# A state-space layer and a gated MLP on one core: ten loads move to GpSimd's queue, and TensorE multiplies a constant in gaps that the planner foresees

## The chip, the cores and the metric

The kernel runs on one core of a Trainium2 chip. The core has five engines that run side by side, each with its own queue of instructions: TensorE (PE, matrix products into PSUM), VectorE (DVE), ScalarE (ACT), GpSimd (POOL) and SyncE (SP, which here only issues transfers). Sixteen DMA engines move data. Transfers are issued by SP, ScalarE or GpSimd, and an issue stands in its engine's queue like any other instruction: what is behind it waits for it.

The metric is the time of one execution on the device in microseconds (us), the median of several runs.

## What is computed

An input `u` of 2048 tokens x 448 channels goes through two blocks, each with a layer norm that is scaled and shifted by rows of `silu(c) @ w_mod`:

```python
mod = (silu(c) @ w_mod).reshape(1, 6, 1, -1)          # sa, ca, ga, sb, cb, gb
h = layernorm(x) * (1 + ca) + sa
x = x + ga * S4(h)                                     # long convolution along the tokens
h = layernorm(x) * (1 + cb) + sb
x = x + gb * ((gelu(h @ w_gate) * (h @ w_up)) @ w_down)
# S4: K[d, l] = Re sum_n C[d,n] dB[d,n] exp(dt A)[d,n]^l ; y = irfft(rfft(K) * rfft(u)) + u * Dskip
```

with 448 channels, 256 states and an inner width of 1792.

## The kernel before

The work falls into stages that overlap.

1. **Start** (to about 50 us). `mod_row` multiplies the broadcast `silu(c)` with a third of `w_mod`'s rows at a time: load `fg` by SP (`m.ld`, L763), four matrix products of 448 columns (`m.mm`, L768), copy by ScalarE (`m.ev`, L771). Meanwhile VectorE and ScalarE prepare the first quarter of the kernel's parameters (`prep`), ScalarE stores them as `lh` (`p.put`, L520) and loads them back in another layout as `lt` (`lt0`, `lt1`, L575). The normalised input goes through a first DFT stage (`ua`, L832).
2. **Main stage** (to about 376 us). For 56 groups of channels: exponents and angles as matrix products (`x.mm` L593, `y.mm` L612, `ang`/`anc` L630), exponential and sine on ScalarE, products on VectorE (`tx`, `tyc`, `tys`, L679 to L687), sums on TensorE (`kgen`, L710; `ka`, L735). Between these run the DFT of the input and, by groups of channels, that of the kernel with the product and the way back (`k_fft`).
3. **Last group of the convolution** (376 to 399 us), `t_fft`: `t.fwd` L1069, `t.p0`/`t.p1` L1075 and L1078, `t.inv` L1085, then a copy out of PSUM (`t.z`, by ScalarE or VectorE), a store of `y` (`t.st`, SP, L1093) and loads of it in another layout (`yi.l0` by SP and `yi.l1` by GpSimd, L1154). For the last, small piece the copy goes straight from tile to tile in single rows (`yi.d00` to `yi.d11`, L1166, issued by SP, ScalarE and GpSimd).
4. **The first block of 512 tokens enters the MLP** (399 to 422 us), `conv_out`: `co.mm` L1246/L1251, the residual and the norm's sums on VectorE (`co.add`), `co.n` L1288/L1289, transposition on TensorE (`co.t`, L1294/L1296), and two half-precision parts (`co.h` on ScalarE or VectorE, `co.l`, L1304).
5. **MLP** (422 us to the end). Weights are loaded in blocks of 256 columns (`w.ld`, L1187, 512 KB each, two a block), split in two half-precision parts (`w.hi` L1195 on ScalarE, `w.lo` L1199/L1200 on VectorE), stored for the later blocks of tokens (`wr.st`, L1209) and used (`gu2`, `gu`, L1371/L1365). Then `dn` (L1441, L1472) with the down weights (`d.ld`, L1547).

**The planner.** Nothing is ordered by hand. Each step is a `Task` with a cost on its engine, a due time `v`, the tasks it depends on, and the buffers that it takes and uses. `Plan.order` places the tasks one at a time: it takes the engine that can start something first, and among the tasks that could start there within 0.25 us (at once on ScalarE) the one with the lowest `v`. The result is the program's order for every engine. `LEAD` adds a constant to the due times of each kind of task (several constants share the tasks of a kind out in order), and `LEAN` is what a start on VectorE is made dearer by, where a task may run on ScalarE or VectorE. A transfer ends, in the plan, after all transfers before it at 280 KB a us; it may start only when the eighth transfer before it, of those issued by SP and ScalarE, has ended (`lanes`). At 0.3 us from engine to engine (`HOP`) this gives planned times; the chip only keeps the order.

Three places that the change touches wait for the end of the main stage (`EV["end"]`): the load of the first residual rows (`x1.ld`, L1120), three constants (`c.ai`, `c.id`, `c.ih`, L414) and the first weights. The first three blocks of weights (`PRE = 3`) are allowed before the MLP begins:

```python
gate = EV["end"] if cb < PRE else CO[0][1]
hold = [YO[2, 2]] if cb < 1 else YL      # a store of y; all loads of yi
t1 = add("w.ld", {"SP": 0.42}, v - 3, ld, [EV["end"]] + hold, [wb], kb=540)
```

Of the kernel before, what the change touches and what calls it, by code (L numbers as in the profile page):

```python
# [41 lines left out]
    "c.ai": (71.008,), "c.ak": (31.634,), "c.au": (64.741,), "c.ea": (129.571,), "c.id": (-5.74,), "c.ih": (81.5,),  # L42
    "c.ld": (-70.212,), "c.rd": (36.588,), "co.add": (126.534,), "co.adde": (-479.654,), "co.addl": (177.332,),
    "co.addx": (510.429, 276.254, 263.838, 306.027), "co.c2": (-16.462, 185.363, 68.605, 81.504),
    "co.h": (1287.071, 1321.404), "co.h2": (-57.238, -19.565, -34.416, 62.618), "co.l": (166.825, 99.971),
    "co.l2": (-304.102, -376.884, -381.167, -327.959), "co.mm": (1047.13,), "co.mme": (35.95,),
    "co.mml": (321.391,), "co.mmx": (504.891, 504.282, 510.751, 509.801), "co.n": (-32.018, -300.752),
    "co.nx": (-309.183, -245.328, -200.245, -90.738), "co.rc": (52.991, 384.121), "co.rcx": (915.491,),
    "co.rt": (-12.141, 45.958), "co.rtx": (-618.711,), "co.t": (505.324, 339.683),
    "co.t2": (-464.884, -636.939, -578.467, -639.884),  # L50
    "cos": (-96.053, -141.432, -54.911, -135.117, -68.696, -62.333),
# [6 lines left out]
    "dt": (81.074,), "e.f": (-100.312, 117.922), "e.hi": (227.13, 344.995), "e.ld": (-39.805, -1.088),  # L58
    "e.lo": (8.272, -319.182), "ev.end": (-23.435,), "ev.fp": (-187.94,), "ev.geg": (-67.509,), "ev.ub": (109.206,),
    "f.fc": (-74.649, -73.839, -55.611, 15.224, 63.434, 91.147),  # L60
# [6 lines left out]
    "gu": (497.845, 500.786, 503.249, 509.096, 515.626, 545.649),  # L67
    "gu.g": (-625.109, -552.414, -602.197, -714.965, -686.389, -501.12), "gu.h0": (645.72, 522.69),
    "gu.ha": (-729.389, -596.515, -731.42, -528.62, -704.301, -709.342),
    "gu.hs": (-239.586, -121.625, -135.62, -164.459, -9.293, -189.977), "gu.l0": (-16.693, -130.465),  # L70
    "gu.la": (-265.608, -410.165, -336.957, -514.583, -455.359, -305.327),
    "gu.ls": (191.831, 190.571, 255.197, 314.456, 219.503, 228.103),
    "gu.m": (114.811, 93.18, 25.848, 285.848, 134.211, 151.44),
# [22 lines left out]
    "sin2": (46.891, 86.759, 111.859, -3.781, 88.196, 21.274), "t.fc": (52.17, 4.168), "t.fwd": (-57.224, -139.59),  # L96
    "t.inv": (-32.42, 14.481), "t.p0": (-56.821, 45.808), "t.p1": (-115.221, 1.658, 219.974, -99.911),
    "t.st": (5.684, 132.896), "t.u": (-64.85, -19.41), "t.z": (101.922, 155.786),
    "tx": (-52.929, -36.943, 40.099, -29.624, 27.922, 13.415),
# [5 lines left out]
    "ub.st": (171.069, 76.93), "ub.u": (-80.805, 32.953), "w.hi": (47.827, -108.842, 52.672, -16.405),  # L105
    "w.ld": (-16.684, 35.68, 34.326, 174.065), "w.lo": (33.536, 32.676, -41.147, -28.811), "warm": (-47.271,),
    "wr.ld": (118.569, -172.29, -6.657, 0.537, 11.936, 73.483), "wr.st": (-77.265, -16.436),
    "x.exp": (-46.635, 7.137, 2.518, -127.479, -61.616, -65.308), "x.ld": (-9.142,), "x.ld0": (-42.934,),
    "x.ld1": (-8.964,), "x.mm": (-1.652, -1.606, -1.613, -1.701, -1.664, -1.631), "x1.ld": (17.13, -239.16),
    "y.exp": (29.939, 99.375, 54.648, -1.232, -161.973, 74.141),  # L110
    "y.mm": (-1.933, -1.54, -1.223, -1.275, -1.525, -1.518), "yi.d00": (-147.672,), "yi.d01": (-171.741,),
    "yi.d10": (-130.853,), "yi.d11": (-32.365,), "yi.e": (-88.98,), "yi.l0": (-123.965, 88.548),
    "yi.l1": (-88.669, -10.274), "yi.ld": (196.171,),
}
LEAN = {
# [5 lines left out]
    "t.z": (5.831, 10.31), "ua.ev": (-0.145, -0.075, 0.628, 8.093, -0.059, 1.101),  # L121
# [29 lines left out]
class Plan:  # L151
# [106 lines left out]
    def run(self):  # L258
        for t in self.order():
            t.fn(t.on) if len(t.eng) > 1 else t.fn()  # L260
# [89 lines left out]
def s4_geglu(ctx: ExitStack, tc: tile.TileContext, a: dict, out: bass.AP):  # L350
# [60 lines left out]

    def sp(n, v, dst, src, kb, deps=(), alloc=(), use=(), q="SP"):
        qf = adma if q == "ACT" else dma
        return add(n, {q: 0.42 if q == "SP" else 0.1}, v, lambda: qf(dst(), src()), deps, alloc, use, kb=kb)  # L414
# [168 lines left out]
    def exps(sc, lt):  # L583
        ss = list(range(sc * SUBS, (sc + 1) * SUBS))
        for k in range(0, SUBS, 2):
# [3 lines left out]
            def xmm(grp=grp, pb=pb):  # L589
                pb.tile = gen.tile([128, 1024], FT, name="pg")  # L590
                for m, s in enumerate(grp):
# [10 lines left out]
            t1 = add("x.mm", {"PE": 0.17 * len(grp)}, v, xmm, [lt, c_rd], [pb, mb], [LT[sc]])  # L602
            t2 = add("x.exp", {"ACT": 0.92 if len(grp) > 1 else 0.6}, v, xact, [t1], (), [pb, mb], table=EXP)
# [91 lines left out]
    def kgen(s, deps):  # L695
        m = s // 2
# [3 lines left out]
        def go():  # L700
            if s % 2 == 0:
                KG[m].tile = kgp.tile([128, 4, 128], FT, name="kg")
            kg = KG[m].tile
# [9 lines left out]
        return add("kgen", {"PE": 1.04}, s, go, list(deps) + [KGT.get(s - 1) if s % 2 else None],  # L713
                   [KG[m]] if s % 2 == 0 else [], [TX[s], TY[s]] + ([KG[m]] if s % 2 else []))
# [43 lines left out]
    def mod_row(i, dst, v, sc=1.0, bs=0.0, deps=()):  # L758
# [5 lines left out]

        def mm():
            pb.tile = fft.tile([128, D], FT, name="pf")
            for t in range(4):
                T.matmul(pb.tile, c_sb[:, t:t + 1].to_broadcast([DT, 128]), wb.tile[:, t], start=(t == 0), stop=(t == 3))  # L768
        t1 = add("m.ld", {"SP": 0.42}, v, ldw, deps[2:], [wb], kb=803)
        t2 = add("m.mm", {"PE": 3.22}, v, mm, [t1, t_si], [pb], [wb])  # L770
        return add("m.ev", {"ACT": 0.46}, v, lambda: A.activation(dst, pb.tile, AF.Copy, scale=sc, bias=bs),  # L771
# [42 lines left out]
    def u_norm_a(jb, v, rst):  # L814
        so = {}
        for jj in range(4):
# [11 lines left out]
            def mm(j=j, pbs=pbs):  # L828
                for h in range(2):
                    pbs[h].tile = fft.tile([128, D], FT, name="pf")  # L830
# [292 lines left out]
    def VB(blk):  # L1123
        return 58.5 if blk == 0 else 100.0 + 20.0 * blk - 20.0
# [519 lines left out]
```

## Time and profile before

| | |
|---|---|
| median of 3 runs | 823.77 us (823.62, 823.77, 831.2) |
| the profiled execution, own time | 825.18 us |
| its span (first to last instruction) | 823.4 us |
| mean granted TensorE clock | 0.969 |
| TensorE, VectorE, ScalarE busy | 748.4, 599.6, 470.3 us |
| GpSimd busy | 6.0 us, 14 instructions |
| transfers by SP and ScalarE's queues | 135.4 MB; by GpSimd's 0.26 MB |

Rows of the timeline read: start, duration (of several instructions: from the first to the last), engine, line, operation, output <- input, count, and in brackets the idle time before with what ended it. A name with q (SPq, ACTq) is an issue on that queue. The chain of waits lists start, duration and what the end of the kernel hung on. A table of stages lists busy time and count of each engine, then the granted TensorE clock, the share of the DMA engines and GB/s. Records of fp32 products come two to a product.

### The profile page before, as it was taken

What the parts mean: (1) busy time and instruction counts of PE and PEld (TensorE: products, weight loads), DVE (VectorE), ACT (ScalarE), POOL (GpSimd) and SP (SyncE); (2) the same over time, 40 slices, a digit from 0 to 9 for tenths busy, and PEclk for the clock granted to TensorE, in tenths of its full rate; (3) what the DMA queues carried; (4) which work ended last, traced back from release to release, by engine and by line L of the source; (5) the groups of instructions that cost most, each with busy time, mean ns of one, the idle gap of its engine ahead of it and who ended that gap; (6) DMA issues with size and microseconds to landing.
All of it is one profiled execution on the core that took longest, in us unless ns stands there. A gap on an engine that the chain in (4) does not pass through costs nothing.

```text
span 823.4 us, 19059 instructions
## 1 busy us (share of the span) xinstructions
PE 748.4 (91%) x8166; PEld 461.2 (56%) x8166; DVE 599.6 (73%) x981; ACT 470.3 (57%) x629; POOL 6.0 (1%) x14
## 2 busy tenths in 40 slices
PE   2786789999799999998589999999999999999997
PEld 1344344444577767778466445444496445864477
DVE  7789998999889989897494783178863686244542
ACT  5598999899968999971244553034442353113320
POOL 0000000000000000000200000000000000000000
PEclk9888799999999999999889999999999999999999
DMA  9552369996858846899669756245315322022101
GB/s 283 148 167 92 105 189 236 285 273 200 236 146 257 233 133 193 253 307 295 189 197 298 267 179 179 75 140 166 117 53 146 135 91 90 34 79 90 45 12 35
DMA packets 92526, 136.83 MB, mean 166 GB/s; under 512 B 21280, under 2 KB 75200, under 8 KB 92442
## 3 DMA queue, kind: packets, MB, share of 16 engines
q1 hardware_dynamic: 89514, 133.75, 53.8%
q10 hardware_dynamic: 2608, 1.61, 0.8%
q8 instruction: 64, 1.05, 0.5%
q0 software_dynamic: 320, 0.26, 0.1%
q14 instruction: 20, 0.16, 0.1%
HBM read 100.48 MB, written 36.01 MB: 166 GB/s over the span
## 4 chain that ended last, share of the span: by engine, by line
PE 67%; ACT 12%; DVE 10%; DMA 6%; issue 3%; SPq 1%; DVEq 0%; ACTq 0%
PE pq L1371 30%; PE pq L1472 9%; PE pd L1441 3%; PE kg L710 3%; ACT fg L643 2%; PE pg L630 2%; PE pf L999 2%; PE pq L1365 2%; PE pf L768 2%; ACT my L617 2%; PE pf L1085 2%; PE pf L895 2%; DVE tx L679 2%; DMA fg<-in_w_mod 2%; PE pd L1472 1%
## 5 line engine op out<-in xcount | busy, mean ns | idle before, releaser
L1371 PE MATMUL pq<-ht,wr 128*128 128x512 f16 (+1 forms) x1200 | 250.0, 367 | 0.0
L1371 PEld LDWEIGHTS <-wr 128*128 128x128 f16 x1200 | 115.4, 98 | 128.6 <-issue 11.0
L1378 ACT ACTIVATE ge<-pq 128x512 f32<-128x512 f32 (+1 forms) x60 | 33.9, 568 | 144.5 <-PE pq L1365 93.9
L1385 DVE TENSOR_TENSOR fq<-ge,pq 128x512 f32<-128x512 f32 (+1 forms) x60 | 38.5, 649 | 72.1 <-PE pq L1371 48.2
L1397 ACT ACTIVATE hh<-fq 128x1024 f16<-128x1024 f32 (+1 forms) x49 | 47.1, 963 | 54.5 <-DVE fq L1385 41.8
L1472 PE MATMUL pq<-d,hh 128*128 128x224 f16 x504 | 73.2, 259 | 0.0
L710 PE MATMUL kg<-ty,tx 128*32 128x64 f32 x3584 | 61.8, 221 | 11.3 <-DVE ty L687 6.4
L679 DVE TENSOR_TENSOR tx<-mx,fg 128x1024 f32<-128x1024 f32 x56 | 68.0, 1220 | 4.0 <-ACT fg L654 2.2
L683 DVE TENSOR_TENSOR ty<-my,fg 128x1024 f32<-128x1024 f32 x56 | 68.2, 1219 | 3.0 <-PE kg L710 2.8
L710 PEld LDWEIGHTS kg<-ty,tx 128*32 128x32 f32 x3584 | 53.0, 110 | 27.6 <-issue 11.2
L1472 PE MATMUL pq<-d,hlo 128*128 128x224 f16 x252 | 65.3, 259 | 0.0
L1400 DVE TENSOR_TENSOR hlo<-fq,hh 128x1024 f16<-128x1024 f32 (+1 forms) x49 | 53.9, 1104 | 5.3 <-ACT hh L1397 5.0
L643 ACT ACTIVATE fg<-pg 128x1024 f32<-128x1024 f32 x56 | 56.6, 1019 | 1.9 <-issue 1.2
L1472 PEld LDWEIGHTS <-hh 128*128 128x128 f16 x588 | 56.7, 98 | 1.1 <-issue 0.4
L617 ACT ACTIVATE my<-pg 128x1024 f32<-128x1024 f32 x56 | 55.3, 1041 | 3.1 <-PE pg L612 2.9
L999 PE MATMUL pf<-q,fc 128*128 128x160 f32 x264 | 42.9, 313 | 0.3 <-DVE q L989 0.3
L630 PEld LDWEIGHTS <-lt 64*128 64x128 bf16 x336 | 20.7, 95 | 37.4 <-issue 20.7
L999 PEld LDWEIGHTS pf<-q,fc 128*128 128x128 f32 x264 | 37.7, 195 | 6.3 <-issue 3.3
L630 PE MATMUL pg<-ea,lt 64*128 64x512 bf16 x168 | 34.9, 389 | 6.2 <-ACT fg L643 4.4
L687 DVE TENSOR_TENSOR ty<-my,fg 128x512 f32<-128x512 f32 x56 | 38.4, 686 | 0.0
L686 DVE SCALAR_TENSOR_TENSOR ty<-my,fg 128x512 f32<-128x512 f32 x56 | 38.4, 685 | 0.0
L735 PE MATMUL kg<-ak,ke 128*64 128x128 f32 x448 | 32.1, 284 | 6.2 <-DVE ke L730 4.4
(172 smaller groups left out, 1196.3 us busy)
## 6 DMA issues: line engine op xcount, KB each, us to landing
wr<-w_d SPq DMA_DIRECT2D x21, 896.0 KB
fc<-in_k_fc SPq DMA_DIRECT2D x20, 576.0 KB
u_d<-so SPq DMA_DIRECT2D x32, 224.0 KB
w<-in_wgu SPq DMA_DIRECT2D x14, 512.0 KB
ui<-u_d SPq DMA_DIRECT2D x10, 672.0 KB
w_d<-wr SPq DMA_DIRECT2D x7, 896.0 KB
fq<-in_wd SPq DMA_DIRECT2D x14, 448.0 KB
us<-uo SPq DMA_DIRECT2D x22, 240.0 KB
```

Of the source, the lines that this page charges most:

```text
L617: A.activation(yb.tile.rearrange("p a b c -> p (a b c)"), pb.tile, AF.Exp)
L630: T.matmul(pa[:, nh * 512:nh * 512 + 512], w, x, start=(k == 0), stop=(k == 2))
L643: A.activation(fb.tile[:, 0].rearrange("p x (n k) -> p n x k", n=2), pb.tile.rearrange("p (n x k) -> p n x k", n=2, x=2), AF.Sin, scale=TW ...
L679: V.tensor_mul(tx.tile, xb.tile[:, xm, None, :].to_broadcast([128, 2, 512]), fb.tile[:, :, 0])
L683: V.tensor_mul(ty.tile[:, 1], yb.tile, fy()[:, 1, :, None, :].to_broadcast([128, 16, 2, 32]))
L710: T.matmul(kg[32 * g:32 * g + 32, 2 * (s % 2) + q, :64], tx[:, r, nh, 4 * q + g], ty[:, r, nh, 4 * q + g], start=(r == 0 and nh == 0), sto ...
L999: T.matmul(pz.tile[:, e % 32 - sl0], fc.tile[:, i, 1 + t], pp.tile[:, t, i], start=(t == 0 and e != 32), stop=(t == 1 and e != 0))
L1371: T.matmul(pb[k].tile[:, ts], wr.tile[:, 4 * lo + t, k, c0:c0 + 128], ht[:, m, ts], start=f % 2 == 0 and i == 0, stop=f % 2 == 1 and i == 9)
L1385: V.tensor_mul(to if half is None else to[:, half:half + 1], *src)
L1397: A.activation(hg.tile[0][:, cb, c], fq.tile[:, c], AF.Copy)
L1400: V.tensor_sub(hg.tile[1][:, cb, c], fq.tile[:, c], hg.tile[0][:, cb, c])
L1472: T.matmul(bank(k)[:, m], x[:, p, q[0], ts], w[:, p, q[1]], start=new and m == 0 and p == 0 and z == 0, skip_group_check=True, stop=i in ( ...
```

## The change

1. The first three blocks' weights (six loads, now `w.lp`), the first block's residual rows (`x1.lp`) and the constants `c.ai`, `c.id` and `c.ih` are issued by GpSimd. The first block's weights no longer wait for a store of `y`; those of blocks 2 and 3 still wait for all loads of `yi`.
2. `Plan.run` notes for each TensorE task how long TensorE is idle before it in the plan. `spin` issues products of the constant `eps` (128 x 128) with itself (up to 448 columns, fp32) into the task's own PSUM tile ahead of its real products: one for each 0.78 us of that idle time beyond 1.5 us. It stands before `x.mm`, every second `kgen`, `m.mm`, `ua`, `co.mm` and `co.t`.
3. `LEAD` and `LEAN` have other values for the kinds of the last stages; those of the main stage are the same. Of the start only the constants' differ.

```diff
 LEAD = {
-    "c.ai": (71.008,), "c.ak": (31.634,), "c.au": (64.741,), "c.ea": (129.571,), "c.id": (-5.74,), "c.ih": (81.5,),
-    "c.ld": (-70.212,), "c.rd": (36.588,), "co.add": (126.534,), ... "co.l": (166.825, 99.971),
+    "c.ai": (-45.617,), "c.ak": (24.994,), "c.au": (41.949,), "c.ea": (33.018,), "c.id": (41.212,),
+    "c.ih": (245.897,), "c.ld": (-43.371,), "c.rd": (51.369,), "co.add": (122.248,), ... "co.l": (-18.313, 59.876),
-    "t.st": (5.684, 132.896), ... "w.lo": (33.536, 32.676, -41.147, -28.811), "yi.d00": (-147.672,), "yi.d01": (-171.741,),
+    "t.st": (-110.71, 72.815), ... "w.lo": (94.634, 7.656, -188.373, -55.953), "yi.d00": (-200.43,), "yi.d01": (-176.155,),
 LEAN = {
-    "t.z": (5.831, 10.31),
+    "t.z": (5.0, -1.486),
...
     def run(self):
+        free = 0.0
         for t in self.order():
+            if t.on == "PE":
+                t.idle, free = t.start - free, t.start + t.eng["PE"]
             t.fn(t.on) if len(t.eng) > 1 else t.fn()
...
+    def spin(me, dst, w=D):
+        for _ in range(int(max(0.0, me[0].idle - 1.5) / (0.78 * w / D))):
+            T.matmul(dst, eps.to_broadcast([128, 128]), eps.to_broadcast([128, w]), start=True, stop=True)
...
     def sp(n, v, dst, src, kb, deps=(), alloc=(), use=(), q="SP"):
-        qf = adma if q == "ACT" else dma
-        return add(n, {q: 0.42 if q == "SP" else 0.1}, v, lambda: qf(dst(), src()), deps, alloc, use, kb=kb)
+        qf = {"ACT": adma, "SP": dma, "POOL": P.dma_start}[q]
+        return add(n, {q: 0.42 if q == "SP" else 0.6}, v, lambda: qf(dst(), src()), deps, alloc, use, kb=kb)
...
         def mm():
             pb.tile = fft.tile([128, D], FT, name="pf")
+            spin(me, pb.tile)
             for t in range(4):
                 T.matmul(pb.tile, c_sb[:, t:t + 1].to_broadcast([DT, 128]), wb.tile[:, t], ...)
...
-            dma(xb.tile, a["A_u"][blk])
-        return add("x1.ld", {"SP": 0.42}, VB(blk) - 5, go, deps, [xb], kb=918)
+            (dma if blk else P.dma_start)(xb.tile, a["A_u"][blk])
+        return add("x1.ld" if blk else "x1.lp", {"SP": 0.42} if blk else {"POOL": 0.6}, VB(blk) - 5, go, deps, [xb], kb=918)
...
-            dma(wb.tile, a["wgu"][cb, :, k])
+            (P.dma_start if cb < PRE else dma)(wb.tile, a["wgu"][cb, :, k])
         gate = EV["end"] if cb < PRE else CO[0][1]
-        hold = [YO[2, 2]] if cb < 1 else YL
-        t1 = add("w.ld", {"SP": 0.42}, v - 3, ld, [EV["end"]] + hold, [wb], kb=540)
+        hold = [] if cb < 1 else YL
+        t1 = add("w.ld" if cb >= PRE else "w.lp", {"SP": 0.42} if cb >= PRE else {"POOL": 0.6}, v - 3, ld, [EV["end"]] + hold, [wb], kb=540)
...
-    c_ai = sp("c.ai", 58, lambda: K2["ai"], lambda: a["k_ai"], 32, [EV["end"]])
+    c_ai = sp("c.ai", 58, lambda: K2["ai"], lambda: a["k_ai"], 32, [EV["end"]], q="POOL")
```

More of the change, by code (lines that the diff above doesn't have):

```diff
@@ L58 @@
-    "dt": (81.074,), "e.f": (-100.312, 117.922), "e.hi": (227.13, 344.995), "e.ld": (-39.805, -1.088),
-    "e.lo": (8.272, -319.182), "ev.end": (-23.435,), "ev.fp": (-187.94,), "ev.geg": (-67.509,), "ev.ub": (109.206,),
-    "f.fc": (-74.649, -73.839, -55.611, 15.224, 63.434, 91.147),
+    "c.ai": (-45.617,), "c.ak": (24.994,), "c.au": (41.949,), "c.ea": (33.018,), "c.id": (41.212,),
+    "c.ih": (245.897,), "c.ld": (-43.371,), "c.rd": (51.369,), "co.add": (122.248,), "co.adde": (-357.4,),
+    "co.addl": (223.45,), "co.addx": (522.285, 249.425, 164.532, 345.011),
@@ L695, in kgen @@
     def kgen(s, deps):
-        m = s // 2
+        m, me = s // 2, []
         if s % 2 == 0:
@@ L712, in go @@
                                      tile_position=(0, 32 * g))
-        return add("kgen", {"PE": 1.04}, s, go, list(deps) + [KGT.get(s - 1) if s % 2 else None],
-                   [KG[m]] if s % 2 == 0 else [], [TX[s], TY[s]] + ([KG[m]] if s % 2 else []))
+        me.append(add("kgen", {"PE": 1.04}, s, go, list(deps) + [KGT.get(s - 1) if s % 2 else None],
+                      [KG[m]] if s % 2 == 0 else [], [TX[s], TY[s]] + ([KG[m]] if s % 2 else [])))
+        return me[0]
     AKB = [Buf("ak%d" % (g % 2)) for g in range(3)]
@@ L1524, in down @@
         out_("6", (0,), 1, 0, [p4], 0.7)
-    c_ai = sp("c.ai", 58, lambda: K2["ai"], lambda: a["k_ai"], 32, [EV["end"]])
-    c_id = sp("c.id", 58, lambda: K2["id"], lambda: a["k_id"], 64, [EV["end"]])
-    c_ih = sp("c.ih", 58, lambda: K2["ih"], lambda: a["k_ih"], 32, [EV["end"]])
+    c_ai = sp("c.ai", 58, lambda: K2["ai"], lambda: a["k_ai"], 32, [EV["end"]], q="POOL")
+    c_id = sp("c.id", 58, lambda: K2["id"], lambda: a["k_id"], 64, [EV["end"]], q="POOL")
+    c_ih = sp("c.ih", 58, lambda: K2["ih"], lambda: a["k_ih"], 32, [EV["end"]], q="POOL")
     t_x = x1_load(0, [EV["end"]])
```

76 lines of the change are left out of this document (44 added, 32 removed), and 21 rows, old and new, of tables (LEAD, LEAN).

## The prediction

> **What bounds the kernel now.** I read the 40 slices first, then the chain of waits in order of time, then a table of stages, then the rows of the two stages that the chain points at.
>
> ```profile
> PE   2786789999799999998589999999999999999997
> PEclk9888799999999999999889999999999999999999
> ...
> core 0: us, PE busy (x) PEld busy (x) DVE busy (x) ACT busy (x) POOL busy (x), PEclk, DMA share, GB/s
> 16.00:22.00 6.00, 6.00 (x8) 2.79 (x9) 4.55 (x10) 0.22 (x1) 0.00 (x0) 1.00 0.88 262
> 32.00:50.00 18.00, 14.93 (x60) 7.13 (x57) 15.78 (x32) 15.47 (x21) 0.00 (x0) 0.62 0.62 162
> 98.00:376.00 278.00, 258.28 (x4759) 168.78 (x4756) 252.61 (x363) 250.82 (x319) 0.00 (x0) 0.99 0.78 229
> 376.00:399.00 23.00, 22.46 (x200) 22.32 (x201) 17.27 (x27) 6.39 (x11) 2.96 (x5) 1.00 0.91 246
> 399.00:410.00 11.00, 1.24 (x9) 0.43 (x8) 4.53 (x8) 2.42 (x4) 2.82 (x5) 0.74 0.53 163
> 410.00:422.00 12.00, 8.70 (x57) 5.78 (x58) 10.42 (x25) 6.13 (x10) 0.00 (x0) 0.78 0.59 200
> 422.00:527.00 105.00, 104.85 (x636) 57.10 (x635) 60.33 (x97) 40.30 (x57) 0.00 (x0) 0.99 0.66 205
> 527.00:823.40 296.40, 291.62 (x1937) 175.00 (x1934) 170.73 (x299) 91.17 (x127) 0.00 (x0) 1.00 0.28 90
> ```
>
> From 98 to 376 us three engines work at once (TensorE 258 of 278 us, VectorE 253, ScalarE 251): nothing is waited for long, so a late start there is carried to the end and an early one too. From 422 us on TensorE is busy 104.85 of 105 us and 291.62 of 296.4: what comes before 422 sets the end, one for one. So only three places can give something: the start, the low clock in the stages 32:50 and 410:422 (0.62 and 0.78), and the hole at 399:410, where TensorE has 1.24 us of work.
>
> The chain of waits at the start, and four rows of the timeline beside it:
>
> ```profile
> 2.63 13.19 DMA fg<-in_w_mod
> 15.96 12.27 PE pf L768 x24
> 28.33 4.86 DMA lt<-lh_d
> 33.24 1.39 PE pg L612 x4
> ...
> 0.81 0.06 DVE L371 MEMSET small<- 128x1 f32 x1 [0.81 <-PEq L1632]
> 20.00 0.42 DVE L473 TENSOR_TENSOR lh<-q,lh 112x256 bf16<-112x256 f32 x1
> 22.30 0.34 ACTq L520 DMA_DIRECT2D lh_d<-lh  x1
> 28.25 0.54 ACT L771 ACTIVATE gs<-pf 128x448 f32<-128x448 f32 x1 [1.84 <-PE pf L768]
> ```
>
> L768 is 12 multiplications, 24 records. The first 8 take 6.0 us (row 16:22), the other 16 the next 6.3 (12.27 in all). The clock column says 1.00 there, but the records say half speed for the first 6 us. The ScalarE queue holds the transfer of lt behind the last of the three copies L771, so lt leaves when L768 ends.
>
> **The start.** The planned idle time before the first L768 follows from the planner's own numbers: 60 + 3 x 224 + 2 x 896 + 784 KB (in its units 61 + 759 + 1836 + 803) at 280 a us are 12.4 us, with 0.4 of issue, 1.5 of landing and 0.3 of hop 14.6 us. int((14.6 - 1.5) / 0.78) is 16 products, 32 records of the shape of L768. If the clock rises after 6.0 us of work as above, 8 records take 6.0 and 24 take 24 x 0.39 = 9.4: 15.4 us. They need only the constant that VectorE writes at 0.81, so they end near 16.3, beside the transfer that lands at 15.8. L768 then starts 0.4 late at most and takes 24 x 0.39 = 9.4 us in place of 12.27. Gain 2.9 - 0.4 = 2.5 us. The transfer lt also needs the store of lh, which ScalarE issues behind the first L771, at 22.30; that copy comes 3 us sooner too, and the data are ready at 20.4, so it doesn't hold.
>
> From L768's end at 28.2 to the first L612 at 33.2 TensorE has little to do; a planned gap of 4 us before the first L832 would give three more products and keep the clock up. The chain from 33 to 45 us runs on TensorE at half speed:
>
> ```profile
> 34.63 1.49 PE pf L832 x4
> 36.55 2.22 PE pf L832 x4
> 39.28 3.77 ACT L617 ACTIVATE my<-pg 128x1024 f32<-128x1024 f32 x4 [1.68 <-PE pg L612]
> 45.44 5.77 DMA xt<-in_A_u
> ```
>
> With L612 of the chain, these TensorE pieces are 5.1 us; at full speed 2.6. But ScalarE idles only 1.68 us there and then bounds the stage, so I take 1.5. Together 4.0 us, all ahead of the stage at 98:376, whose order the change leaves as it is. Ends: 0 (another transfer holds the stage) and 2.9 + 2.6, so 5.5. In this stage the change also sends ea before rd; rd's first reader, L593, comes after ea's, L612, so this costs nothing.
>
> [...]
>
> **The hole at 399:410.**
>
> ```profile
> SPq L1166 <- DMA yi<-zo: 2.5, 1, 2.5
> SPq L1166 <- DMA w<-in_wgu: 1.5, 1, 1.5
> ...
> 395.49 0.43 SPq L1187 DMA_DIRECT2D w<-in_wgu  x1
> 400.51 3.72 SPq L1166 DMA_DIRECT2D yi<-zo  x2
> 404.28 0.57 SPq L1093 DMA_DIRECT2D y<-lh  x1
> ...
> 407.70 0.56 POOL L1154 DMA_DIRECT2D yi<-y  x1 [2.77 <-DMA y<-lh]
> 410.23 1.32 PE L1251 MATMUL pd<-yi,ai 128*64 128x128 f32 x8 [9.99 <-DMA yi<-y]
> ```
>
> The last results go ScalarE, store y (L1093), load yi (L1154), L1251. The last store stands in SP's queue behind the direct copies L1166. Those waited 1.5 us for a first weight w to land (L1187) and 2.5 us for another direct copy: the planner counts eight outstanding transfers of SP and ScalarE together, and counting back eight from the first L1166 on SP in the program's order one reaches that weight. The change takes the weights off these queues: the 1.5 us go, and two of SP's issues with them. The rest hangs on the order. The preference of t.z to VectorE moves from 10.3 against it to 1.5 for it, so the last two copies run on VectorE, 0.28 us apart by the planner, just over its choice window of 0.25, and the store should go ahead of L1166. It would leave near 400.0 in place of 404.28. I take 4.0 us; ends 0 and 6 (the two transfers behind it, 3.4 us from store to load and 2.5 from load to L1251, might be some 0.9 us shorter each without the weights' traffic beside them).
>
> What moves to GpSimd: one load of x, three constants and six weights (the first two without their former wait). They stand ahead of eight L1154 and the two L1166 of that queue.
>
> ```profile
> L1154 POOL DMA_DIRECT2D yi<-y x8: 557/564/723, 392.8 to 407.7; - x8
> L1166 POOL DMA_DIRECT2D yi<-zo x2: 543/545/547, 399.7 to 400.2; - x2
> 376.66 0.73 SPq L414 DMA_DIRECT2D ident<-in_k_id  x1
> ```
>
> A GpSimd issue costs 0.56 us for 8 rows and 0.545 for one: hardly by rows. By that slope 128 rows are 0.9 us; in proportion to rows they would be 9. I take 0.9: from 376.7 six issues (x, constants, two weights) are done by 383, before the first L1154 at 392.8: GpSimd's idle time hides them. Above 2.7 us each the cover is gone and the L1154 move out; the last of them, with some 5.6 us of the queue's own issues ahead of it, comes later than now from 4.2 us each. The other four weights wait, as before, for all yi loads. ScalarE and VectorE get the splitting of the first two weights sooner, inside 376:399; both have slack there (6.39 and 17.27 us busy of 23). Without that slack it would cost VectorE's two pieces, 2.8 us by the rows below.
>
> [...]
>
> **From 410 to 422.**
>
> ```profile
> 420.11 0.95 DVE L1199 SCALAR_TENSOR_TENSOR wr<-w,wr 128x768 f16<-128x768 f32 x1
> 421.07 0.42 DVE L1200 SCALAR_TENSOR_TENSOR wr<-w,wr 64x256 f16<-64x256 f32 x1
> 421.52 0.69 DVE L1304 TENSOR_TENSOR ht<-pq,ht 128x512 f16<-128x512 f32 x1
> 421.54 3.92 PE L1371 MATMUL pq<-ht,wr 128*128 128x256 f16 x20
> 425.72 2.36 PE L1371 MATMUL pq<-ht,wr 128*128 128x256 f16 x20
> ```
>
> VectorE bounds this stretch: 10.42 of 12 us. The second L1304 (the row here), which releases the first L1371, stands behind a weight's 1.38 us and behind the sums of later rows. By the due times the change turns this round: co.l 262 to 77, w.lo 94 to 155, co.add 223 to 219. With one instruction in progress each time I take 2.0 us; ends 0 and 3.5.
>
> The same 20 L1371 take 3.92 us and, 4 us on, 2.36: the first at half clock. With products in the hole the clock may stay up: 1.5 us; ends 0 and 2.2 (half of L1251's 1.32 with it).
>
> ```profile
> 404.00:405.00 1.00, 0.00 (x0) 0.65 0.13 43
> ```
>
> Here the clock fell about 4 us after the last product (410.23 - 9.99 = 400.2). Products fill the front of a planned gap, 0.39 us a record; in a wait of 6 us five of them end 2 us before L1251 and the clock holds. In one of 10 us it falls.
>
> **After 422** TensorE has no idle time to win. What was ahead by 10 us needs its weights sooner, in a stage with a DMA share of 0.66:
>
> ```profile
> 493.98 6.34 DMA fq<-in_wd
> ```
>
> The load of the last down weights stands on the chain of waits: they arrive just as they are needed. I give back 1.0 us; ends 0 and 4.
>
> **Sum**: -4.0 - 4.0 - 2.0 - 1.5 + 1.0 = -10.5 us. The profiled execution took 825.18 us (span 823.4 and 1.8 around it), 1.4 above the median of 823.77 (823.62 to 831.2). So 814.7 against the profile's own time, **813.3 against the median**; its own range is 808 to 818.
>
> **Rivals.**
> 1. *The hole stays* (0.20). The store still stands behind L1166, or the 2.5 us wait for the direct copy lasts. For it: L1166 has kept a far earlier due time. Then the products end over 3 us before L1251, the clock falls, and 4.0 and 1.5 are lost: 823.8 - 4 - 2 + 0.5 = 818.3. [...]
> 2. *The start isn't carried* (0.12): the load of x at 45.44 or the transfers at 150 to 200 us hold the stage. Against it: they are issued on release. 823.8 - 6.5 = 817.3.
> 3. *Slower: the clock doesn't rise under constant products* (0.05). Place: before L768. 32 records at 0.75 us take 24 us, L768 starts at 24.9, 8.9 late, and the hole's (at most ten, for a planned gap as long as the wait now: 15 us) end 5 us past L1251's start. 823.8 + 8.9 + 5 - 2 = 835.7. It decides from a cold time over 6 us, and eats the gain of 3 at 12 us. Against it: L768 itself has a constant first operand and the clock rose.
> 4. *Slower: GpSimd's issue goes by rows* (0.02), 9 us each: six end at 430.7, the last L1154 leaves near 436.3 in place of 407.7. 823.8 + 28.6 - 4 - 2 = 846. It decides from 4.2 us each; the two rows above speak against it.
> 5. *More than forecast* (0.08): ends of hole and start together, 806.
> That the change adds no products is a small part of rival 1: only gaps above 2.28 us get one.
>
> **How the numbers follow.** Forecast 0.52. The range runs from 807 to 822: rivals 1 and 2 lie inside, half of 5, and 3 and 4 outside. 1% is 8.2 us, about what a measurement here can tell from no change: faster means below 815.5. The likelier two thirds of the forecast's range lie there (0.35), with 0.08 from 5 and some of 1 and 2 (0.06): 0.49. Slower over 832 (rivals 3 and 4, less a part that comes out milder): 0.06. Within: 0.45.
>
> **What would show it.** The first L768 about 9.4 us long and lt issued near 25.8; about 16 products ahead of it; clock near 1.00 in 30 to 48 us. The same work at 98:376 some 4 us sooner. On SP no L1187 before 400, L1093 ahead of L1166, L1251 near 402 (406 less the start's 4). L1371's first 20 at 2.4 us. Wrong would be: L1251 still 10 us after the last L1246; idle TensorE in 422:527 over 3 us; L768 at 24.

## The result and the profile after

The changed kernel takes 822.58 us in the median of 20 runs (820.07 to 826.22), the kernel before 825.55 us beside it (820.12 to 831.76). The ratio is 0.9948 with a 95% interval of 0.9928 to 0.9967: 4.3 us less. The ratio is estimated from fast runs alone and is not the quotient of the two medians, which is 0.9964 (3.0 us less). Timed a second time it was 0.9973 (0.9944 to 1.0001), 2.2 us less. The forecast was 10.5 us less, 813.3 us, with a range of 807 to 822: the direction is right, the size is not, and the time lies just outside the range.

The profiled execution took 822.29 us (span 820.5). In the changed kernel the line numbers are L418 for the products of the constant, L785 for the former L768, L853 for L832, L624 for L612, L723 for L710, L1115 for L1093 (store y), L1176 for L1154 (load yi), L1188 for L1166 (single-row copies), L1209 for L1187 (weights), L1107 for L1085, L1271/L1276 for L1246/L1251 and L1401 for L1371. The 40 slices of its page:

```profile
PE   9786889999899999989789999999999999999997
PEclk9998798999999999999999999999999999999999
```

Its table of stages, with the columns as before (time, busy time and count of PE, PEld, DVE, ACT and POOL, granted clock, DMA share, GB/s):

```profile
16.00:22.00 6.00, 6.00 (x17) 3.03 (x16) 4.50 (x10) 2.70 (x5) 0.00 (x0) 1.00 1.02 273
32.00:50.00 18.00, 13.19 (x65) 5.91 (x62) 14.63 (x32) 15.51 (x21) 0.00 (x0) 0.84 0.67 193
98.00:130.00 32.00, 27.58 (x523) 15.06 (x512) 30.38 (x51) 29.76 (x44) 0.00 (x0) 0.89 0.79 209
200.00:240.00 40.00, 37.90 (x734) 24.80 (x735) 38.73 (x58) 36.73 (x45) 0.00 (x0) 1.00 0.75 210
399.00:410.00 11.00, 6.16 (x46) 4.92 (x47) 2.16 (x9) 1.01 (x3) 1.69 (x4) 0.84 0.76 250
410.00:422.00 12.00, 9.74 (x73) 6.80 (x70) 11.18 (x23) 4.38 (x8) 0.69 (x2) 0.86 0.14 45
```

and two rows of the same table of the kernel before, which the forecast did not look at:

```profile
98.00:130.00 32.00, 27.40 (x611) 15.54 (x608) 29.95 (x54) 31.66 (x45) 0.00 (x0) 1.00 0.77 214
200.00:240.00 40.00, 34.37 (x601) 21.89 (x600) 33.63 (x52) 32.67 (x41) 0.00 (x0) 0.96 0.59 171
```

The start runs faster: 17 records of TensorE in 16:22 where 8 stood, and a clock of 0.84 in 32:50 where 0.62 stood. But between 200 and 240 us TensorE does 3.5 us more in the same time, though the change puts nothing there; and the hole 399:410 is still there, now with products in it (they are its 6.16 us), and with a DMA share of 0.76 in place of 0.53. The chain of waits of the changed kernel, start and hole:

```profile
9.81 6.42 PE pf L418 x17
16.23 9.04 PE pf L785 x24
...
26.12 5.03 DMA lt<-lh_d
31.19 1.03 PE pg L624 x2
```

```profile
395.39 0.29 DVE zo L414
395.69 0.25 SPq L1115
396.04 0.64 SPq L1188
...
399.93 0.68 SPq L1176
400.65 5.53 DMA yi<-y
...
406.74 0.91 PE pd L1276 x4
...
416.02 3.12 PE pq L1401 x16
```

The 16 products end at 16.2, L785 takes 9.04 us in place of 12.27, and the L624 of the chain starts at 31.19, where L612 started at 33.24. In the hole the store L1115 now goes ahead of the copies L1188, and SP waits for no weight any more. What holds L1276 is the landing of the last load of yi: 5.53 us from its issue. The row of the kernel before, and what GpSimd and TensorE do in the changed kernel at that time (timeline):

```profile
407.64 2.45 DMA yi<-y
```

```profile
395.03 6.86 PE L418 MATMUL pd<-small 128*128 128x128 f32 x60
399.58 1.15 POOL L1209 DMA_DIRECT2D w<-in_wgu  x2
401.34 0.43 SPq L1231 DMA_DIRECT2D w_d<-wr  x1
415.79 0.53 POOL L1209 DMA_DIRECT2D w<-in_wgu  x1 [15.06 <-DVE wr L1222]
443.01 1.69 PE L1401 MATMUL pq<-ht,wr 128*128 128x512 f16 x7 [0.69 <-DVE wr L1222]
```

GpSimd issues two weights of 512 KB at 399.58, while SP is still issuing its last three loads of yi (399.14 to 401.3). Of the four weights of blocks 2 and 3 only these two are under way then; the other two are issued at 415.79 and 421.84. The products end at 401.9, 4.8 us before L1276.

### The profile page after: what moved, and what is told of

The parts are those of the page before. It is cut to its first block, busy times and chain, and to the rows that moved or that the text cites. A ratio compares the mean times of both kernels' runs of the same rounds, so it can differ in the third digit from the quotient of the medians.

```text
span 820.5 us, 19281 instructions
## 1 busy us (share of the span) xinstructions
PE 769.6 (94%) x8264; PEld 472.9 (58%) x8264; DVE 600.3 (73%) x983; ACT 470.3 (57%) x627; POOL 11.3 (1%) x24
## 4 chain that ended last, share of the span: by engine, by line
PE 66%; ACT 12%; DVE 12%; DMA 4%; issue 4%; SPq 1%; ACTq 0%; DVEq 0%
PE pq L1401 30%; PE pq L1502 9%; PE pd L1471 4%; ACT fg L655 3%; PE kg L723 2%; PE pg L642 2%; PE pq L1395 2%; PE pf L418 2%; PE pf L917 2%; PE pf L1021 2%; DVE tx L691 2%; ACT fg L647 2%; DVE ty L695 2%; PE pd L1502 1%; PE pf L785 1%
## 5 line engine op out<-in xcount | busy, mean ns | idle before, releaser
L1401 PE MATMUL pq<-ht,wr 128*128 128x512 f16 (+1 forms) x1200 | 250.7, 367 | 3.3 <-DVE ht L1333 1.2
L1401 PEld LDWEIGHTS <-wr 128*128 128x128 f16 x1200 | 114.9, 98 | 132.5 <-issue 14.0
L723 PE MATMUL kg<-ty,tx 128*32 128x64 f32 x3584 | 62.1, 222 | 8.0 <-DVE ty L699 7.6
L723 PEld LDWEIGHTS kg<-ty,tx 128*32 128x32 f32 x3584 | 53.3, 111 | 24.3 <-DVE ty L699 11.0
L1021 PEld LDWEIGHTS pf<-q,fc 128*128 128x128 f32 x264 | 36.5, 190 | 6.1 <-issue 3.0
```

The source lines that it names most:

```text
L723: T.matmul(kg[32 * g:32 * g + 32, 2 * (s % 2) + q, :64], tx[:, r, nh, 4 * q + g], ty[:, r, nh, 4 * q + g], start=(r == 0 and nh == 0), sto ...
L1021: T.matmul(pz.tile[:, e % 32 - sl0], fc.tile[:, i, 1 + t], pp.tile[:, t, i], start=(t == 0 and e != 32), stop=(t == 1 and e != 0))
L1401: T.matmul(pb[k].tile[:, ts], wr.tile[:, 4 * lo + t, k, c0:c0 + 128], ht[:, m, ts], start=f % 2 == 0 and i == 0, stop=f % 2 == 1 and i == 9)
```

## The experiments

Differences are (ratio - 1) times the median of the kernel before, timed beside it on the same chip. Kernels called "of before" have the order and the due times of the kernel before. Their line numbers are shifted by a few; the operation and the tiles tell which line it is. A single profile says little about a difference of a few us: the kernel of before with all products starts the last product of the last group at 390.66 us in one profiled execution and at 395.03 in another.

| kernel | ratio, 95% interval | against before |
|---|---|---|
| changed kernel; timed again | 0.9948 (0.9928 to 0.9967); 0.9973 (0.9944 to 1.0001) | -4.3; -2.2 us |
| of before, first products only | 0.9930 (0.9905 to 0.9955) | -5.8 |
| of before, 16 tiny products | 0.9962 (0.9936 to 0.9987) | -3.1 |
| of before, 64 products of one by one | 1.0040 (1.0009 to 1.0072) | +3.3 |
| of before, products of the start | 0.9891 (0.9841 to 0.9940) | -9.0 |
| of before, all products; again | 0.9866 (0.9829 to 0.9903); 0.9903 (0.9867 to 0.9939) | -11.1; -8.0 |
| same, ten loads by GpSimd | 0.9919 (0.9887 to 0.9952) | -6.7 |
| same as "all products", store ahead | 0.9867 (0.9823 to 0.9910) | -11.0 |
| same, with six loads by GpSimd | 0.9854 (0.9825 to 0.9883) | -12.1 |
| changed, no products | 1.0064 (1.0038 to 1.0091) | +5.3 |
| changed, no products, weights 2 and 3 by SP | 0.9996 (0.9967 to 1.0026) | -0.3 |
| changed, products of the start only | 0.9932 (0.9905 to 0.9958) | -5.6 |
| changed, weights 2 and 3 by SP | 0.9863 (0.9825 to 0.9902) | -11.3 |
| changed, splitting late | 0.9899 (0.9872 to 0.9925) | -8.4 |
| changed, both | 0.9888 (0.9849 to 0.9927) | -9.3 |

**Products and order apart.** Four kernels separate them.

```diff
 # changed kernel, no products
-        for _ in range(int(max(0.0, me[0].idle - 1.5) / (0.78 * w / D))):
+        for _ in range(0 * int(max(0.0, me[0].idle - 1.5) / (0.78 * w / D))):
 # changed kernel, products of the start: spin returns at once for co.mm and co.t
 # of before, first only: spin returns at once for all but m.mm
 # of before, all products: spin as changed; LEAD, LEAN and the queues as before
```

> The kernel before, order and queues untouched, with the products of the constant ahead of the first L768 only (16 of them). Theory A (the start's gain of 2.6 us is carried through the main stage to the end): 2.0 to 2.6 us less than the kernel before, and the exponents' stage starts 2 to 3 us sooner. Theory B (the main stage has slack that swallows it, as the two profiles seem to say at 122 to 134 us, where 2.0 of 2.2 us are lost): 0 to 0.5 us less. Theory C (the forecast's sum): 4.0 less.

> The kernel before, order and queues untouched, with all products: 16 ahead of the first L768, some three ahead of an L832, and those of the planned gaps ahead of the last piece's co.mm and of co.t. Theory A: like the run with the first products alone within 0.5 us (the clock falls again before the hole's end, so its products give nothing). Theory C: another 1.5 us less than that run, by the clock at L1371.

> The changed kernel, order and queues the same instruction for instruction, without any product of the constant. Theory A: about 2 us less than the kernel before (order and queues alone), 2.3 more than the changed kernel. Theory B: as fast as the changed kernel, 4 us less than before. Theory C: order and queues give 5.0 less than before.

> The changed kernel with the products of the start (ahead of the first L768 and of an L832) but none ahead of co.mm and co.t. Theory A: within 0.5 us of the changed kernel (4.3 us less than before), since the clock falls in the hole with them too. Theory C: 1.5 us more than the changed kernel, the first 16 records of L1401 at 3.9 us instead of 3.1.

No theory had this right. The products in the old order give 11.1 us, more than any expectation; order and queues alone cost 5.3 us, where all three theories had them a gain of 2 to 5. In the changed order the products ahead of co.mm and co.t give nothing that can be measured (-5.6 without them, -4.3 with them); without them the first 16 records of L1401 even ran at the full clock in the profiled execution, 1.91 us where theory C had 3.9 (timeline):

```profile
417.65 1.91 PE L1403 MATMUL pq<-ht,wr 128*128 128x256 f16 x16 [0.97 <-DVE ht L1335]
```

And the first products give 5.8 us, where the theories had 0 to 4.0.

**A part of the start's gain is not warmth.** In the two kernels without products (before, and changed without them) the stretch from the 35th to the 39th copy L617 took 41.5 and 41.7 us, in the four with products 36.3 to 36.5. The timeline of the kernel before shows why, and the summary of its transfers between 223.5 and 227 us:

```profile
221.67 1.88 PE L710 MATMUL kg<-ty,tx 128*32 128x64 f32 x107
226.93 0.86 PE L710 MATMUL kg<-ty,tx 128*32 128x64 f32 x21 [3.38 <-issue]
```

```profile
DMA packets 32, 0.14 MB, mean 40 GB/s; under 512 B 14, under 2 KB 14, under 8 KB 31
q8 instruction: 1, 0.02, 1.9%
```

TensorE stands 3.38 us in the middle of one group of 128 equal products. It waits for no semaphore ("issue"); the transfers are few, and one of them is a block of 16 KB of instructions. It starts at 224.45, after TensorE has stopped, takes 1.09 us, and TensorE goes on at 226.93. Two kernels test whether the place where such a block ends decides.

```diff
 # of before, 16 tiny products ahead of the first L768
-            T.matmul(dst, eps.to_broadcast([128, 128]), eps.to_broadcast([128, w]), ...)
+            T.matmul(dst[:, :1], eps.to_broadcast([128, 128]), eps, ...)
 # of before, 64 products of one by one
+        for _ in range(4 * int(...)):
+            T.matmul(dst[:1, :1], eps, eps, ...)
```

> The kernel before with 16 products of one column each ahead of the first L768: TensorE gets as many instructions more as with the 16 products of 448 columns, but too little work to raise its clock. The stretch from 216 to 257 us took 41.5 us in the two kernels without products at the start (before, and the changed kernel without products) and 36.4 us in the four with them; in the slow ones TensorE stands 3.4 us inside one group of L710, with no semaphore to wait for, while its instructions are fetched. Theory A (the products shift where TensorE's blocks of instructions end; warmth has no part in it): that stretch takes 36 to 37 us, the start gains nothing, and the whole is 3 to 5 us less than the kernel before. Theory B (the earlier start or the warm clock does it): the stall stays, and the time is that of the kernel before within 1 us.

> The kernel before with 64 products of one by one ahead of the first L768, 256 instructions of TensorE, as many as one fetched block of 16 KB holds if an instruction has 64 bytes. Theory A (the place of the blocks' ends decides): the stall inside the group of L710 is back, at the same record of the group (after some 107 of 128), the stretch from 216 to 257 us takes 41 to 42 us, and the time is that of the kernel before within 1.5 us. Theory B (any products at the start remove it): no stall, 36 to 37 us, 3 us less than before as with 16.

With 16 tiny products the group has no such stop (its 128 records, timeline), the stretch takes 36.3 us, and 3.1 us are gained although L768 (first row) still takes 11.65 us, so nearly cold:

```profile
13.84 11.65 PE L786 MATMUL pf<-fg,pk 112*128 112x448 f32 x24 [5.93 <-DMA fg<-in_w_mod]
...
224.65 1.10 PE L724 MATMUL kg<-ty,tx 128*32 128x64 f32 x64
226.25 1.10 PE L724 MATMUL kg<-ty,tx 128*32 128x64 f32 x64 [0.49 <-DVE ty L700]
```

With 64, which are 256 instructions more (128 multiplications and as many loads of weights), the stall is back after the same record, the 107th:

```profile
223.67 1.75 PE L724 MATMUL kg<-ty,tx 128*32 128x64 f32 x107
228.38 0.53 PE L724 MATMUL kg<-ty,tx 128*32 128x64 f32 x21 [2.96 <-issue]
```

That settles it: theory A. (The stretch takes 39.5 us, not 41 to 42: the 21 records behind the stall took 0.53 us, where they took 0.86 in the kernel before, whose clock was 0.50 from 226.80 to 230.22. The whole is 3.3 us more than before, 1.8 more than was expected.) All eighteen profiles sort the same way: before, the 64 products and the two changed kernels without products stand 2.96 to 3.50 us inside this group, after 106 or 107 of its records; the other fourteen, with 64 or 76 instructions more at the start, don't, and their stretch takes 36.3 to 38.2 us. That it is back with 256 agrees with a count in the profile of the kernel before: 64 transfers of instructions on q8, 1.05 MB, for 16332 records of multiplications and loads of weights on TensorE, so 16 KB and 255 records each (an estimate that puts all of q8 down to TensorE; 65 for 16528 in the changed kernel, 254 each). Why this block, of the many, is asked for only after TensorE has stopped is not shown.

The first full-size products against the tiny ones, 5.8 to 3.1 us, leave 2.7 us for warmth, but each of the two intervals is 4 us wide, so this is not resolved. The profile of the tiny products can't settle it either: there fg landed 2.1 us sooner (L768 from 13.84, before from 15.96). The three ahead of an L832 were tried in the old order with the first 16, nothing else:

```diff
 # of before, products of the start: spin returns at once for co.mm and co.t
```

> The kernel before with the products of the start only, those ahead of the first L768 and of an L832; none in the hole. Before, this job's like: 5.8 us less with the first alone, 11 less with all. Theory A (the three products ahead of an L832 give about 1 us, those of the hole some 1 to 3 by the clock at L1371): 6.5 to 8 us less than the kernel before. Rival E (the hole's products give the whole difference): 5.8 less. Rival F (they give nothing, the difference is spread of the runs): as fast as with all products.

9.0 us less than before: 3.2 more than the first alone gave, 0.5 short of all products (9.5, the mean of 11.1 and 8.0). The intervals are 3 to 4 us wide on each side; neither step is resolved, and so E and F stay open.

**What the order and the queues cost.** Candidates were the four weights of blocks 2 and 3 on GpSimd, and the splitting of the first block's weights inside the last group.

```diff
 # of before, all products, ten loads by GpSimd at their old places in the order (x and the constants likewise)
-            dma(wb.tile, a["wgu"][cb, :, k])
+            (P.dma_start if cb < PRE else dma)(wb.tile, a["wgu"][cb, :, k])
 # changed, weights 2 and 3 by SP (with and without products)
-            (P.dma_start if cb < PRE else dma)(wb.tile, a["wgu"][cb, :, k])
+            (P.dma_start if cb < 1 else dma)(wb.tile, a["wgu"][cb, :, k])
 # changed, splitting late: the first two w.hi and w.lo set behind yi.d11 in the list of tasks
```

> The kernel before with all products, and the ten loads issued by GpSimd at their old places in the program's order (the due times are those of before). Measured against the run with the products alone (11 us less than before). Theory A (the weights of blocks 2 and 3 share the DMA engines with the last loads of yi, the splitting of the first block's weights is where it was): the last yi lands 2 to 3 us later after its issue, but L1187's wait for w goes; together within 1.5 us of the products alone. Theory C (the forecast): the hole shrinks by the 1.5 us of the wait for w. Theory D (the queue is what costs the 5 us of the changed kernel without products): 4 to 5 us more than the products alone.

> The changed kernel with the splitting of the first block's weights (two w.hi, two w.lo) put behind the last group's pieces, where it stood before; all else as changed. Theory A (VectorE bounds the last group, and these two w.lo, 2.8 us, stand in its way): the stretch from the first t.fwd to the last t.inv falls from 25.5 to 22 to 23 us and the time by 2 to 3 us against the changed kernel. Rival: the stage is slow for another reason (the order of its pieces), and the time stays within 1 us.

> The changed kernel with the four weights of blocks 2 and 3 issued by SP again (so behind the last loads of yi), x, the constants and the first two weights by GpSimd as changed; the planner's order is the same. Theory A (those weights share the DMA engines with the last loads of yi): the last yi lands 2.3 to 3 us after its issue in place of 5.5, the first L1276 comes 2.5 to 3 us sooner, and the time is 2 to 3 us less than the changed kernel's. Rival: another load takes the place, the time stays within 1 us.

> The changed kernel with both: the splitting of the first block's weights put back behind the last group's pieces, and the weights of blocks 2 and 3 by SP. Theory A (the two costs add): 6 to 7 us less than the changed kernel, about the time of the kernel before with all products (11 us less than before). Rival: the two overlap, 4 us less than the changed kernel, as with the splitting alone.

> The changed kernel without any product and with the weights of blocks 2 and 3 issued by SP again. Theory A (these weights are most of what the order and the queues cost): the hole from the last L1085 to the first L1251 falls from 12.1 to 8.5 to 9.5 us, and the time from 5.3 us more than the kernel before to 0.5 to 2.5 more. Rival: the new order itself costs it, the time stays above 4 us more than before.

The landing of the last load of yi in the chains of waits: changed kernel timed again, changed without products; then the same two with the weights by SP.

```profile
399.63 5.64 DMA yi<-y
```
```profile
410.72 5.92 DMA yi<-y
```
```profile
399.58 2.44 DMA yi<-y
```
```profile
406.92 2.46 DMA yi<-y
```

Behind SP's own loads of yi the weights leave from 400.33 on (with products) and disturb nothing: 2.4 us in place of 5.5 to 5.9, and the hole from the last L1107 to the first L1276 is 8.7 us in place of 11.8 (8.95 and 12.1 without products). In time the kernel without products goes from +5.3 to -0.3 us, the changed kernel from -4.3 to -11.3. Each pair's intervals lie apart. So the queue of the four weights is the cost of the order and the queues, all of it that can be measured. The profiles account for some 3.5 us from the last L1107 to the end, 3.1 of them the hole; the times differ by 5.6 to 9.1 us (the second timing of the changed kernel gives the 9.1), and what the rest is isn't shown. Moving the queue alone in the old order costs 2.8 us against the mean of the two timings with all products, unresolved by itself; there too SP has issued the last yi by 401.3 and L1251 begins only at 406.9 (what the profile names as landing last is a weight of GpSimd's queue, issued at 401.07, 5.70 us). Theory A had the landing right and the size too small.

The splitting stands in VectorE's way as the rows show (changed kernel, timeline), but putting it back doesn't add to the weights' gain (-9.3 with both, -11.3 with the weights alone):

```profile
381.08 0.95 DVE L1221 SCALAR_TENSOR_TENSOR wr<-w,wr 128x768 f16<-128x768 f32 x1
383.90 0.96 DVE L1221 SCALAR_TENSOR_TENSOR wr<-w,wr 128x768 f16<-128x768 f32 x1
```

The last group takes 24.5 us with the splitting late, 25.5 as changed and 22.2 in the kernel before; of the difference 1.3 us are co.mme (L1271), moved into it. Why this kernel alone was 8.4 us faster than before is not explained: its profile shows 1.0 us of that, and the hole as long as in the changed kernel, 11.8 us. The profiled execution was the slowest of its six, 821.74 us.

**The store ahead, by hand, in the old order.**

```diff
+        st = [t for t in o if t.n == "t.st"][-2]
+        o.remove(st)
+        o.insert(min(i for i, t in enumerate(o) if t.n[:4] == "yi.d"), st)
```

> The kernel before with all products; x, three constants and the first block's two weights by GpSimd, the other four weights by SP as before; and the last but one store of y set ahead of the single-row copies L1166 by hand, nothing else moved. Theory A and C: L1166's waits no longer stand ahead of the store, the hole before L1251 shrinks from 12.2 to 8 to 9 us, and the time is 3 to 4 us less than with the products alone. Rival: the direct copies themselves land last, the hole stays above 11 us and the time within 1 us.

> The kernel before with all products, every load on its old queue, and one thing moved by hand: the last but one store of y ahead of the single-row copies L1166. In the run with x, the constants and two weights on GpSimd besides, TensorE waited 0.7 and 2.3 us for the last group's table fg, since x had been asked for earlier. Theory A: fg is in time, the last group takes 22 to 23 us, the hole 10 to 11: 1.5 to 3 us less than with the products alone, 12 to 14 less than before. Rival: the store waits for a free transfer in the same way and nothing is gained.

With the loads on their old queues the store goes at 390.88, and SP then stands at the copies L1191 until another copy has landed (timeline, and a row of the chain):

```profile
390.88 0.36 SPq L1118 DMA_DIRECT2D y<-lh  x1
395.52 2.53 SPq L1191 DMA_DIRECT2D yi<-zo  x4
```
```profile
389.87 5.59 DMA yi<-zo
```

The hole stays at 13.0 us and the time at -11.0: the rival. With x, the constants and the first weights on GpSimd besides, the hole is 10.5 us, but x is then asked for sooner (362.62 us; with all loads on their old queues at 367.94, behind the last table) and the last group waits for its table, as the rows suggest by the same cause, a load on another queue beside one that is needed first:

```profile
371.94 1.13 PE L1094 MATMUL pf<-ako,fg 128*128 128x128 f32 x8 [0.73 <-DMA fg<-in_k_fc]
379.12 1.69 PE L1094 MATMUL pf<-ako,fg 128*128 128x128 f32 x10 [2.25 <-DMA fg<-in_k_fc]
```

-12.1 us, not to be told from -11.0. The two repeats:

> The changed kernel as it is. By the first timing 4.3 us less than the kernel before; by both theories the same again within 1.5 us, and its last yi lands 5 to 6 us after its issue.

> The kernel before with all products, as once before (11.1 us less than before). Theory A: again 9 to 12 less, 5 to 7 less than the changed kernel beside it. Rival (the first timing had few undisturbed runs): within 3 us of the changed kernel.

Beside each other the old order with all products is 5.8 us faster than the changed kernel. Several versions beat both kernels, among them the changed one with the four weights given back to SP (817.88 us, 11.3 less than before), but the data do not rank them.

## Why the prediction was wrong

Step by step:

- **The start, -4.0.** The count of 16 products, their end near 16.3 and the unchanged transfer lt were right, and so was the cold time: eight records at half the pace in 6.08 us, from 0.92 to 7.00 as from 15.96 to 22.04 before; L785 took 9.04 where 9.4 was said, lt landed at 31.1. Times of whole kernels give 2.7 us for the first products' warmth, unresolved. Whether it is carried to the end is not shown, and rival 2 stays open: the thirteen profiles with full-size products at the start begin the 35th copy L617 at 211.9 to 218.7 us, the five without at 213.3 to 220.0. In the changed kernel's first profile the lead is gone by the 20th copy (131.3 us, before 131.4), behind a low stretch of the clock from 123.0 to 129.8 that the row 98:130 shows as 0.89; in its second profile that stretch is missing and the 20th copy starts at 128.8. Rival 3 fell with L785's 9.04 us.
- **Not in the sum at all: 3.1 us** (1.1 to 5.3 by its interval) by the fetch of instructions. The row 200:240 of the profile before held it (34.37 us of TensorE in 40), and I had called 98:376 a stage where nothing is waited for long, from its total of 258 in 278.
- **The hole, -4.0.** This is the step that failed. The store did go ahead of L1166 and the wait of 1.5 us for w is gone, as said. But the step ended at "the other four weights wait, as before, for all yi loads". They do so in the plan. On the chip nothing holds them on GpSimd: before, they stood behind the loads of yi in SP's own queue, and that order was what protected the loads. Now they share the DMA engines with them, 5.53 us for 2.45, at a DMA share of 0.93 while the load is under way (400.65 to 406.18) where it was 0.44 (407.64 to 410.09). I had even counted the absence of their traffic as a possible gain of 0.9 us a transfer. The hole was 11.8 us against 11.5: no gain. With the weights by SP it is 8.7 us, 2.8 less, so the term was also a little large. What the sharing costs I did not price.
- **VectorE's slack in the last group.** The forecast gave the splitting of the first weights no price, because VectorE was busy 17.27 of 23 us. The group takes 25.5 us where it took 22.2: 1.3 are co.mme, 1.0 goes when the splitting is set late, and the rest is not traced.
- **410 to 422, -2.0.** Right in size: from L1276 to the first 16 of L1401 9.3 us, before 11.3. In the way it is half right: the sums of one later row and one norm went behind the second L1333 (the former L1304), but a weight's splitting still stands ahead of it (L1221 at 413.86, L1222 at 414.82).
- **The clock at L1371, -1.5.** Nothing, and the mechanism was wrong too. The low clock under L1371 is not the one of the hole. Tables of stages, the kernel before and then the changed one:

```profile
414.00:421.00 7.00, 3.93 (x32) 2.86 (x28) 6.79 (x15) 4.54 (x8) 0.00 (x0) 0.96 0.45 178
421.00:425.00 4.00, 4.00 (x24) 2.70 (x23) 3.92 (x9) 1.25 (x1) 0.00 (x0) 0.57 0.41 131
```
```profile
409.70:416.50 6.80, 4.54 (x39) 3.15 (x36) 6.61 (x13) 2.20 (x4) 0.53 (x1) 1.00 0.00 0
416.50:419.90 3.40, 3.40 (x20) 1.94 (x18) 3.27 (x8) 1.24 (x2) 0.00 (x0) 0.50 0.50 157
```

  In both kernels the clock had been back up for 6.83 us when it fell a second time, at L1371 (at 421.36) and at L1401 (at 416.53). The second profile of the changed kernel has its 16 records at the full clock, 1.91 us in place of 3.12, and so has the one without the products of the hole; with the weights by SP the first eight records of co.mm behind the hole took 0.88 us, so the full clock, and yet the 16 records took 3.24. So the products don't set it. What they do reach is co.mm. Where they ended 1.7 to 2.4 us ahead of it (three profiles), its first eight records took 0.85 to 0.88 us; from 3.2 us on (seven profiles, the changed kernel with 4.8 among them) 1.32 to 1.34. The weights by SP, then the second profile of the old order with all products:

```profile
402.58 0.88 PE L1276 MATMUL pd<-yi,ai 128*64 128x128 f32 x8 [1.71 <-DMA yi<-y]
```
```profile
406.31 1.32 PE L1275 MATMUL pd<-yi,ai 128*64 128x128 f32 x8 [3.20 <-DMA yi<-y]
```

- **After 422, +1.0.** It was 2.6: the first L1401 (16 records, at 416.02) starts 5.5 us sooner than before, the first group of 40 with 512 columns (445.17, before 448.40) 3.2 us sooner, and the end is 2.9 us sooner. Between them TensorE waits 0.46 and 0.69 us for the splitting of weights (441.50 and 443.01), and two transpositions stand there where one did. GpSimd's last two weights wait for a free tile (15.06 us in the row at 415.79); whether that delays the splitting is not shown.
- **GpSimd's issue** costs 0.58 us for 128 rows (1.15 for two), where the slope gave 0.9 and proportion to rows 9: rival 4 fell.

The products in the old order come to -8.0 to -11.1 us, near the forecast's -10.5, but by another sum: luck. The loss of some 5.6 us by the weights is most of what separates the forecast from the result. Rival 1, the hole that stays, is what came, and its gain of 5.5 us is near the measured 4.3; but it named a store behind L1166 or a wait for a copy, and neither occurred, so that is luck too. Rival 5's 806 doesn't follow from its words: with the far ends of start and hole and the rest of the sum as it stands one gets 809.8.

## What to carry to other kernels

A load that is moved to an idle engine's queue also loses what stood ahead of it in the old queue (here the last load of yi landed after 5.53 us in place of 2.45, and after 2.44 with the weights back on SP): ask which small transfers went first only because of that order, and keep bulk loads behind them by a real dependence or in the same queue. A gap of TensorE that is put down to no semaphore, in a run of equal instructions, is worth a look for a fetched block of instructions; here 64 instructions more upstream took it away and with 256 more it stood at the same record again, so a comparison has to keep their number equal. Products of a constant kept the clock up for the work behind them only where they ended within 2.4 us of it (0.85 to 0.88 us for the first eight records of co.mm; at 3.2 us it was low again, 1.32), and a later stretch fell low all the same (0.50 from 416.53 to 419.94 in the changed kernel).

## What was not expected of the hardware

- A block of TensorE's instructions that arrives late costs 3.0 to 3.5 us (before 3.38, the 64 products 2.96, changed without products 3.50 and 3.23), and was back when 256 instructions were added.
- The granted clock in the traces of both kernels is 1.00 or 0.50, the low stretches 3.41, 6.83, 10.24 or 13.65 us long (but for the last, which the trace's end cuts), and which stretches fall low differs between executions: in the changed kernel 123.0 to 129.8 us in one (the row 98:130 has 0.89), none there in the other.
- 128 records of one by one took 3.34 us (26 ns each), 32 records of 128 x 128 with a single column 6.99 us (218 ns each): with as little as one column to multiply, the record with the larger constant to load took eight times as long.
